# Regrouped filter rows, DMA transposes, normalization on ScalarE and smaller first blocks in a fused spectral and gated-FFN kernel

## The chip, the cores and the metric

The kernel runs on one core of one Trainium2 chip. The metric is the device time of one execution in microseconds (us). A time quoted for a kernel is the median of its runs. A profile is one execution with the hardware profiler on. Its span, from the first to the last instruction, is about 2 us shorter than the device time of the same execution.

The engines are PE (TensorE, matrix multiplications), DVE (VectorE), ACT (ScalarE), POOL (GpSimd) and SP (SyncE, which here only issues DMAs). PEld stands for PE's weight loads. In this program PE writes its results to a memory called PSUM, and the other engines fetch them from there. A transfer *lands* when its data have arrived.

## The reference, cut to what matters

```python
def reference(A_x, A_w_r, A_w_i, B_x, B_w_gate, B_w_up, B_w_down):   # A_x: 1 x 2048 x 512
    xn = _layernorm(A_x)                           # over the last axis
    X  = rfft2(xn);  X = X * (w_r + 1j * w_i)      # filter: 2048 x 257
    spectral = irfft2(X).astype(bf16)
    g  = xn @ w_gate;  u = xn @ w_up               # 512 x 1792 each
    ffn = (gelu(g) * u) @ w_down                   # 1792 x 512
    return A_x + spectral + ffn
```

All tensors are bf16. The kernel computes the Fourier transforms as matrix multiplications with constant tables.

## The kernel before

The 2048 rows are 16 chunks of 128 rows. One *unit* of the FFN (`glu`) makes 128 of the 1792 hidden columns for a block of chunks: 4 matmuls into `g_ps`, 4 into `u_ps`, the gelu on ACT, the product `hT` on DVE. For a block of 4 chunks one unit takes PE about 1.73 us. The other work is placed between the units by a hand-made list of tasks, each with the moment (in us of ideal PE time) at which it is put into the program. An engine runs its own instructions one after the other, near the program's order but not exactly in it: the traces show some places changed (in after, DVE takes the statistics of chunks 2 and 3 before chunk 0's reciprocal, which the program has the other way round). An engine's order below is the one that the trace shows. Cuts are marked with `# ...`.

```python
def layernorm(c0, n):                      # for the n chunks from c0
    for j in range(n):
        nc.vector.bn_stats(out=stats[:, j, :], in_=x_t[:, c0 + j, :])
        nc.vector.bn_aggr(out=mv[:, j, :], in_=stats[:, j, :])
    if c0 < 4:
        nc.scalar.activation(out=rstd[:], in_=mv[:, :, 1], func=AF.Sqrt, bias=eps_t[:], scale=1.0)
        nc.vector.reciprocal(out=rstd[:], in_=rstd[:])
    else:
        rsqrt(rstd, mv[:, :, 1], n)        # 12 small DVE instructions
    for j in range(n):
        nc.vector.tensor_scalar(out=xn[:, c0 + j, :], in0=x_t[:, c0 + j, :],
                                scalar1=mv[:, j, 0:1], scalar2=rstd[:, j:j + 1],
                                op0=ALU.subtract, op1=ALU.mult)

def transposes(c0):                        # two chunks, on PE, copied out of PSUM by DVE
    tp = ps.tile([P, NE, 2, P], BF16, name="tp", tag="S", bufs=4)
    for e in range(NE):
        for j in range(2):
            nc.tensor.transpose(tp[:, e, j, :], xn[:, c0 + j, e * P:(e + 1) * P], ident)
    nc.vector.tensor_copy(out=xnT[c0 // 4][:, :, c0 % 4:c0 % 4 + 2, :], in_=tp[:])
# ...
```

The spectral part folds `xn` by symmetry (`fold`, DVE), transforms along the rows (`pstep` into `bp`, `dstep` into `dp`, `cstep` into `ep`, each a group of matmuls and a cast on ACT), and then, for each of 8 groups g of frequencies, filters on DVE. The filtered tile `F` is shuffled across partitions by four DMAs before PE takes it up again:

```python
def filt(g):
    # ... X from E; two multiplications by the filter's rows, tr and ti
    V.tensor_tensor(out=m1[:]..., in0=Xv, in1=tr, op=ALU.mult)             # 128x1024, L340
    V.tensor_tensor(out=m2[:]..., in0=Xv[:, ::-1], in1=ti, op=ALU.mult)    # 128x1024, L341
    # ... Y and F from them, on DVE
    for h in range(2):
        for r in range(2):
            nc.sync.dma_start(out=F2[64 * r:64 * r + 64, h], in_=F[64 * h:64 * h + 64, r])   # L364
    f_tiles[g] = F2

def icstep(g):                             # back-transform: needs F2
    # ... per half: 4 matmuls into gp, then a cast on ACT to Gs
```

The filter rows are loaded as 28 plain loads and 18 gathers into `TW = [P, 2, NG, 2, 258]`. The program's order:

```python
layernorm(0, 2); transposes(0)
units = [(0, 2, fc) for fc in range(3)]          # the first 4 chunks in blocks of two
for fc in range(NFC):
    units.append((2, 2, fc))
    if fc + 3 < NFC: units.append((0, 2, fc + 3))
for sb in range(1, NSB):
    units += [(4 * sb, 4, fc) for fc in range(NFC)]
tasks = [(0, lambda: layernorm(2, 2)), (0, lambda: transposes(2))]
for cg in range(1, 4):
    t = 4 + 6 * (cg - 1)                         # layernorm at t, its transposes at t + 3
    # ...
for cg in range(4):
    t = 8 + 5 * cg                               # fold at t, the four psteps at t + 2 .. t + 5
    # ...
t0, dt = 32, 6.0
for g in range(NG):
    # dstep at t0 + dt*g and + 1, cstep and filt at + 4
    tasks.append((t0 + dt * g + 11, lambda g=g: icstep(g)))
# ... the units in order, each preceded by the tasks that are due;
# then idstep (into yp) and down (into y_ps), chunk by chunk
```

Of the kernel before, what the change touches and what calls it, by code (L numbers as in the profile page):

```python
# [10 lines left out]
P = 128  # L11
BF16 = mybir.dt.bfloat16
F32 = mybir.dt.float32
# [7 lines left out]
NG = 8  # L21
# [7 lines left out]
def _tables():  # L29
# [14 lines left out]
    p = np.arange(P)[:, None]  # L44
    ka = np.arange(64)[None, :]
    RF = np.zeros((P, NC, 2, 64))
# [49 lines left out]
    RI = np.zeros((2, 64, NC, P))  # L96
    kac = np.arange(64)[:, None]
    pr = np.arange(P)[None, :]
# [6 lines left out]
    def low(a):  # L105
        return a.reshape(P, -1).astype(np.float32).astype(ml_dtypes.bfloat16)


    h, kb, a = np.arange(P) // 64, np.arange(P) // 4 % 16, np.arange(P) % 4
    idx = np.zeros((P, NG, 2), dtype=np.int32)  # L110
    for g in range(NG):
        ks = 8 * g + 4 * h + a + 128 * kb
        if g == 0:
            ks = np.where((h == 0) & (a == 0) & (kb >= 8), 64 + 128 * (kb - 8), ks)
        idx[:, g, 0] = ks
        idx[:, g, 1] = (S - ks) % S
    idx[0, 0, 1] = S // 2
    return low(np.concatenate(parts, axis=1)), cols, low(RF), low(RI), idx.reshape(P, -1)


@with_exitstack
def kernel(
# [36 lines left out]
    late = {}  # L159
    TW = pc.tile([P, 2, NG, 2, 258], BF16, name="TW", tag="TW")  # L160
    TR, TI = TW[:, 0], TW[:, 1]
# [5 lines left out]
    def load_consts(first, last):  # L167
        a, b = ccols[first][0], sum(ccols[last])
        nc.sync.dma_start(out=CT[:, a:b], in_=cap[:, a:b])


    def load_x(c0, n, eng=nc.sync):
        eng.dma_start(out=x_t[:, c0:c0 + n, :], in_=x_v[:, c0:c0 + n, :])

    def load_w(a, b):
        nc.sync.dma_start(out=Wg_sb[:, :, a:b], in_=wg_v[:, :, a:b])
        nc.sync.dma_start(out=Wu_sb[:, :, a:b], in_=wu_v[:, :, a:b])

    load_x(0, 1)
    load_x(1, 1, nc.scalar)  # L180
    load_consts("ident", "ident")
    load_x(2, 2, nc.scalar)
    load_w(0, 256)
    load_w(256, 640)
    load_x(4, 4)
    load_w(640, 1216)
    load_x(8, 4)
    nc.sync.dma_start(out=RF_t[:], in_=rf_d.rearrange("p (c k) -> p c k", c=NC))
    load_w(1216, 1792)
    load_x(12, 4)  # L190
    load_consts("F0", "M0")




    W = 257
    idx_t = pc.tile([P, NG, 2], I32, name="idx_t")
    nc.gpsimd.dma_start(out=idx_t[:], in_=nc.inline_tensor(idx_np, name="spec_rows").ap()
                        .rearrange("p (g s) -> p g s", s=2))
    for T, w_in in ((TR, A_w_r), (TI, A_w_i)):  # L200
        rows = w_in.rearrange("(kb g h a) k -> h g kb a k", kb=NC, h=2, a=4)
        for g in range(NG):
            for s in range(2):
                if g > 0 and s == 0:
                    for h in range(2):
                        nc.sync.dma_start(out=T[64 * h:64 * h + 64, g, 0, 0:W], in_=rows[h, g])
                else:
                    nc.gpsimd.indirect_dma_start(
                        out=T[:, g, s, 0:W], out_offset=None, in_=w_in[:, :],
                        in_offset=bass.IndirectOffsetOnAxis(ap=idx_t[:, g, s:s + 1], axis=0))  # L210
    nc.sync.dma_start(out=Wd_sb[:], in_=wd_v)

# [24 lines left out]
    def layernorm(c0, n):  # L237
        stats = pw.tile([P, n, nc.vector.BN_STATS_DIM], F32, name="stats")
        mv = pw.tile([P, n, nc.vector.BN_AGGR_DIM], F32, name="mv")
        rstd = pw.tile([P, n], F32, name="rstd")  # L240
        for j in range(n):
            nc.vector.bn_stats(out=stats[:, j, :], in_=x_t[:, c0 + j, :])  # L242
            nc.vector.bn_aggr(out=mv[:, j, :], in_=stats[:, j, :])
        if c0 < 4:
            nc.scalar.activation(out=rstd[:], in_=mv[:, :, 1], func=AF.Sqrt, bias=eps_t[:], scale=1.0)
            nc.vector.reciprocal(out=rstd[:], in_=rstd[:])
        else:
            rsqrt(rstd, mv[:, :, 1], n)
        for j in range(n):
            nc.vector.tensor_scalar(out=xn[:, c0 + j, :], in0=x_t[:, c0 + j, :],  # L250
                                    scalar1=mv[:, j, 0:1], scalar2=rstd[:, j:j + 1],
                                    op0=ALU.subtract, op1=ALU.mult)

    def transposes(c0):
        tp = ps.tile([P, NE, 2, P], BF16, name="tp", tag="S", bufs=4)
        for e in range(NE):
            for j in range(2):
                nc.tensor.transpose(tp[:, e, j, :], xn[:, c0 + j, e * P:(e + 1) * P], ident)  # L258
        nc.vector.tensor_copy(out=xnT[c0 // 4][:, :, c0 % 4:c0 % 4 + 2, :], in_=tp[:])

# [26 lines left out]
    def evac(o, i):  # L287
        nc.scalar.copy(out=o, in_=i)  # L288
# [3 lines left out]
    def dstep(G):  # L292
        dp = ps.tile([P, 2, P, 2], F32, name="dp", tag="S", bufs=4)
        for q in range(4):
            nc.tensor.matmul(dp[:, q % 2, :, q // 2], lhsT=Bs[:, q, G].rearrange("p c r a -> p (c r a)"),  # L295
                             rhs=FQ[q], start=(q == 0), stop=(q == 3), skip_group_check=True)
        ds = pw.tile([P, D], BF16, name="ds", bufs=4)
        evac(ds[:], dp[:].rearrange("p s k t -> p (s k t)"))
        ds_tiles[G] = ds
# [14 lines left out]
    def tables_fix():  # L314
        V = nc.gpsimd
        t0 = pc.tile([1, 2, 2], BF16, name="t0")
        V.tensor_scalar(out=t0[0:1, 0, :], in0=TR[0:1, 0, :, 0], scalar1=0.5, scalar2=None, op0=ALU.mult)
        V.tensor_scalar(out=t0[0:1, 1, :], in0=TR[0:1, 0, :, 256], scalar1=0.5, scalar2=None, op0=ALU.mult)
        tt = pc.tile([P, 4, NG], F32, name="tt")
        V.tensor_tensor(out=tt[:, 0], in0=TR[:, :, 0, 0], in1=TR[:, :, 1, 0], op=ALU.add)  # L320
        V.tensor_tensor(out=tt[:, 1], in0=TR[:, :, 0, 256], in1=TR[:, :, 1, 256], op=ALU.add)
        V.tensor_tensor(out=tt[:, 2], in0=TI[:, :, 0, 0], in1=TI[:, :, 1, 0], op=ALU.subtract)
        V.tensor_tensor(out=tt[:, 3], in0=TI[:, :, 0, 256], in1=TI[:, :, 1, 256], op=ALU.subtract)
        for k, (T, s) in enumerate(((TR, 0), (TR, 1), (TI, 0), (TI, 1))):
            V.tensor_scalar(out=T[:, :, s, 0], in0=tt[:, k], scalar1=0.5, scalar2=None, op0=ALU.mult)
        f_tiles["t0"] = t0

    def filt(g):
# [5 lines left out]
        V.tensor_copy(out=X[:, :, 0].rearrange("p (r s) -> p r s", r=2), in_=E[:, :, :, 0])  # L334
        tr = TR[:, g, :, 0:256].unsqueeze(1).to_broadcast([P, 2, 2, 256])
        ti = TI[:, g, :, 0:256].unsqueeze(1).to_broadcast([P, 2, 2, 256])
        m1 = pw.tile([P, 4, 256], BF16, name="m1", bufs=1)
# [12 lines left out]
        if g == 0:  # L350

            u = pw.tile([1, 2, 2, 256], BF16, name="u", tag="A", bufs=1)
            E0, F0 = E[0:1], F[0:1]
            TR0, TI0 = TR[0:1, 0, :, 0:256], TI[0:1, 0, :, 0:256]
            for s, op in ((0, ALU.add), (1, ALU.subtract)):
# [13 lines left out]
    def icstep(g):  # L369
        F = f_tiles[g]  # L370
        if g == 0:
            late["G"] = pc.tile([P, 4, NC, 2, 64], BF16, name="Gs", tag="x_t")
# [73 lines left out]

    layernorm(0, 2)
    transposes(0)
    units = [(0, 2, fc) for fc in range(3)]
    for fc in range(NFC):  # L450
        units.append((2, 2, fc))
        if fc + 3 < NFC:
            units.append((0, 2, fc + 3))
    for sb in range(1, NSB):
        units += [(4 * sb, 4, fc) for fc in range(NFC)]

    tasks = [(0, lambda: layernorm(2, 2)), (0, lambda: transposes(2))]

    for cg in range(1, 4):
        t = 4 + 6 * (cg - 1)  # L460
        tasks.append((t, lambda cg=cg: layernorm(4 * cg, 4)))
        tasks.append((t + 3, lambda cg=cg: transposes(4 * cg)))
        tasks.append((t + 3, lambda cg=cg: transposes(4 * cg + 2)))
    for cg in range(4):
        t = 8 + 5 * cg
        tasks.append((t, lambda cg=cg: fold(cg)))
        for q in range(4):
            tasks.append((t + 2 + q, lambda cg=cg, q=q: pstep(cg, q)))
    tasks.append((20, tables_fix))
    t0, dt = 32, 6.0  # L470
    for g in range(NG):
        tasks.append((t0 + dt * g, lambda g=g: dstep(2 * g)))
        tasks.append((t0 + dt * g + 1, lambda g=g: dstep(2 * g + 1)))
        tasks.append((t0 + dt * g + 4, lambda g=g: cstep(g)))
        tasks.append((t0 + dt * g + 4, lambda g=g: filt(g)))
        tasks.append((t0 + dt * g + 11, lambda g=g: icstep(g)))
    tasks.sort(key=lambda x: x[0])
# [45 lines left out]
```

## Time and profile before

| | before |
|---|---|
| device time, median of 3 runs | 198.14 us (198.07 to 198.33) |
| device time of the profiled run | 217.64 us |
| first `g_ps` matmul in that profile | 9.85 us |
| PE, busy share of the profiled span | 85% |

These are lines of the profile's page for the kernel before. A row has 40 digits, one for each fortieth of the span. A digit is the busy share in tenths. PEclk is the granted TensorE clock in tenths of full speed.

```profile
span 215.6 us, 3193 instructions
...
PE   0581009999889999999999899999999999999993
...
PEclk9998555999999999999999999999999999999999
```

PE is nearly full after a poor start. There is a hole in slices 4 to 6, with the clock at half in slices 5 to 7. This profiled run was 19.5 us longer than the timed ones, so it isn't the timed program.

The chain of waits of the kernel before, near its start (start in us, duration in us, what):

```profile
3.73 1.29 DVE stats L242 x2
...
9.85 1.01 PE g_ps L425 x4
...
16.21 15.92 another core or an unknown queue x2
```

The data of the first chunks land at 3.7 us, and the first FFN matmul starts 6.1 us later. The last line is the hole: 15.9 us that no recorded instruction explains.

The same profile in stretches: the window, its length, then busy us and (instructions) of PE, PEld, DVE, ACT and POOL, the clock, the busy share of the DMA engines, GB/s.

```profile
40.00:50.00 10.00, 9.52 (x97) 7.98 (x96) 9.64 (x33) 4.81 (x12) 0.82 (x4) 1.00 0.66 219
50.00:63.00 13.00, 11.05 (x109) 8.85 (x108) 12.79 (x46) 5.67 (x14) 0.00 (x0) 1.00 0.01 2
```

From 40 to 63 us DVE is busy for 22.4 of 23 us, while PE has gaps. This is the stage with layernorm, fold and the copies of the transposes.

One line from the list of PE's waits (what waited, on what: us in total, times, longest), and one multiplication by the filter's rows of each kind (line, engine, operation, tiles, shapes, count; then busy us, mean ns, and idle us before it):

```profile
PE gp L378 <- DMA F_1361<-F: 0.6, 2, 0.4
```

```profile
L340 DVE TENSOR_TENSOR m_950<-X,TW 128x1024 bf16<-128x1024 bf16 x1 | 0.7, 694 | 0.0
...
L341 DVE TENSOR_TENSOR m_1054<-X,TW 128x1024 bf16<-128x1024 bf16 x1 | 0.7, 686 | 0.0
```

PE waits for the shuffle of F.

### The profile page before, as it was taken

How to read it: one execution, taken by the hardware profiler on the slowest of the kernel's cores; microseconds unless marked ns; L12 is line 12 of the kernel's file. 1: busy time of each engine (PE TensorE's matmuls, PEld its weight loads, DVE VectorE, ACT ScalarE, POOL GpSimd, SP SyncE). 2: the span in 40 equal slices, each digit the busy share in tenths (PEclk: the TensorE clock that was granted, in tenths of full speed). 3: DMA queues.
4: the chain of work that ended last, by engine and by line, in shares of the span. 5: the costliest groups of instructions: out<-in, count | busy, mean ns of one | idle time of the engine just before them, and what ended most of it. 6: DMA issues, size and time to landing. Idle time of an engine off the chain costs nothing.

```text
span 215.6 us, 3193 instructions
## 1 busy us (share of the span) xinstructions
PE 184.0 (85%) x1136; PEld 102.2 (47%) x1136; DVE 126.2 (59%) x316; ACT 90.3 (42%) x170; POOL 20.3 (9%) x33
## 2 busy tenths in 40 slices
PE   0581009999889999999999899999999999999993
PEld 0451006787665545455445445444454444545441
DVE  3970006999998339978578487493353544255421
ACT  2310002353618566787778768754341212121100
POOL 1777740100000000000000000000000000000000
PEclk9998555999999999999999999999999999999999
DMA  5999732760000200101202202202002222222211
GB/s 166 362 382 380 205 76 49 223 213 3 0 2 3 97 0 2 41 19 40 49 0 52 50 0 55 49 0 49 0 3 73 73 73 85 70 91 72 77 49 49
DMA packets 17503, 17.69 MB, mean 82 GB/s; under 512 B 2208, under 2 KB 16304, under 8 KB 17488
## 3 DMA queue, kind: packets, MB, share of 16 engines
q1 hardware_dynamic: 16592, 15.90, 24.1%
q0 software_dynamic: 608, 1.19, 1.9%
q10 hardware_dynamic: 288, 0.39, 0.6%
q8 instruction: 9, 0.15, 0.3%
q14 instruction: 6, 0.05, 0.1%
HBM read 13.29 MB, written 2.10 MB: 71 GB/s over the span
## 4 chain that ended last, share of the span: by engine, by line
PE 57%; DVE 17%; another core or an unknown queue 7%; issue 6%; DMA 5%; ACT 5%; SPq 2%; DVEq 0%
PE y_ps L438 22%; PE u_ps L428 12%; PE g_ps L425 12%; ACT E L310 3%; DVE stats L242 2%; SPq L364 2%; PE tp L258 2%; DVE hT_187 L432 2%; PE dp L295 2%; PE yp L393 2%; PE y_ps L440 2%; DMA x_t<-in_A_x_dram 1%; PE bp L282 1%; DVE hT_1164 L432 1%
## 5 line engine op out<-in xcount | busy, mean ns | idle before, releaser
L431 ACT ACTIVATE ge<-g_ps 128x512 bf16<-128x512 f32 (+1 forms) x70 | 35.4, 517 | 52.2 <-PE g_ps L425 26.3
L428 PEld LDWEIGHTS <-Wu_sb 128*128 128x128 bf16 x280 | 28.3, 101 | 35.2 <-issue 14.9
L425 PEld LDWEIGHTS <-Wg_sb 128*128 128x128 bf16 x280 | 28.6, 104 | 23.2 <-issue 5.2
L443 DVE TENSOR_TENSOR y_sb<-y_ps,y_sb 128x512 bf16<-128x512 f32 x16 | 11.1, 692 | 30.2 <-PE y_ps L440 30.2
L425 PE MATMUL g_ps<-xnT_70,Wg_sb 128*128 128x256 bf16 x112 | 19.4, 300 | 10.5 <-issue 10.5
L428 PE MATMUL u_ps<-xnT_70,Wu_sb 128*128 128x256 bf16 x112 | 18.5, 297 | 7.8 <-DVE hT_187 L432 7.0
L399 ACT CAST yf<-yp 128x512 bf16<-128x512 f32 x16 | 9.2, 587 | 37.3 <-PE yp L393 37.3
L432 DVE TENSOR_TENSOR hT_187<-u_ps,ge 128x256 bf16<-128x256 f32 x28 | 11.6, 419 | 19.6 <-remote 16.0
L310 ACT CAST E<-ep 64x512 bf16<-64x512 f32 x32 | 18.5, 579 | 4.0 <-PE ep L307 3.7
L425 PE MATMUL g_ps<-xnT_72,Wg_sb 128*128 128x512 bf16 x56 | 15.4, 384 | 0.0
L425 PE MATMUL g_ps<-xnT_71,Wg_sb 128*128 128x512 bf16 x56 | 15.0, 381 | 0.0
L425 PE MATMUL g_ps<-xnT_73,Wg_sb 128*128 128x512 bf16 x56 | 14.9, 380 | 0.0
L428 PE MATMUL u_ps<-xnT_72,Wu_sb 128*128 128x512 bf16 x56 | 14.9, 379 | 0.0
L428 PE MATMUL u_ps<-xnT_73,Wu_sb 128*128 128x512 bf16 x56 | 14.9, 379 | 0.0
L428 PE MATMUL u_ps<-xnT_71,Wu_sb 128*128 128x512 bf16 x56 | 14.4, 380 | 0.0
L432 DVE TENSOR_TENSOR hT_807<-u_ps,ge 128x512 bf16<-128x512 f32 x14 | 9.6, 687 | 7.0 <-PE u_ps L428 6.7
L258 PE MATMUL tp<-CT,xn 128*128 128x128 bf16 x64 | 6.5, 243 | 7.7 <-DVE xn L250 7.6
L438 PE MATMUL y_ps<-Wd_sb,hT_187 128*128 128x512 bf16 x56 | 12.7, 379 | 0.0
L438 PE MATMUL y_ps<-Wd_sb,hT_807 128*128 128x512 bf16 x56 | 12.7, 379 | 0.0
L438 PE MATMUL y_ps<-Wd_sb,hT_1164 128*128 128x512 bf16 x56 | 12.7, 379 | 0.0
L242 DVE BATCH_NORM_STATS2 stats<-x_t 128x6 f32<-128x512 bf16 x16 | 10.6, 678 | 3.4 <-DMA x_t<-in_A_x_dram 3.4
L288 ACT CAST Bs<-bp 128x512 bf16<-128x512 f32 x16 | 8.5, 598 | 6.3 <-PE bp L282 6.3
(126 smaller groups left out, 242.0 us busy)
## 6 DMA issues: line engine op xcount, KB each, us to landing
y_sb<-in_A_x_dram SPq DMA_DIRECT2D x16, 128.0 KB
out_dram<-y_sb SPq DMA_DIRECT2D x16, 128.0 KB
Wd_sb<-in_B_w_down_dram SPq DMA_DIRECT2D x1, 1792.0 KB
x_t<-in_A_x_dram SPq DMA_DIRECT2D x3, 512.0 KB
Wg_sb<-in_B_w_gate_dram SPq DMA_DIRECT2D x2, 576.0 KB
Wu_sb<-in_B_w_up_dram SPq DMA_DIRECT2D x2, 576.0 KB
RF_t<-spec_rf SPq DMA_DIRECT2D x1, 512.0 KB
RI_t<-spec_ri SPq DMA_DIRECT2D x1, 512.0 KB
```

The source lines that it names most:

```text
L242: nc.vector.bn_stats(out=stats[:, j, :], in_=x_t[:, c0 + j, :])
L258: nc.tensor.transpose(tp[:, e, j, :], xn[:, c0 + j, e * P:(e + 1) * P], ident)
L288: nc.scalar.copy(out=o, in_=i)
L295: nc.tensor.matmul(dp[:, q % 2, :, q // 2], lhsT=Bs[:, q, G].rearrange("p c r a -> p (c r a)"), rhs=FQ[q], start=(q == 0), stop=(q == 3), ...
L310: nc.scalar.copy(out=E[64 * h:64 * h + 64, r], in_=ep[64 * r:64 * r + 64])
L399: nc.scalar.copy(out=yf[:, c % 2], in_=yp[:])
L425: nc.tensor.matmul(gp[:], lhsT=Wg_sb[:, e, fc * P:(fc + 1) * P], rhs=rhs[:, e, :], start=(e == 0), stop=(e == NE - 1))
L428: nc.tensor.matmul(up[:], lhsT=Wu_sb[:, e, fc * P:(fc + 1) * P], rhs=rhs[:, e, :], start=(e == 0), stop=(e == NE - 1))
L431: nc.scalar.activation(out=ge[:], in_=gp[:], func=AF.Gelu_apprx_tanh)
L432: nc.vector.tensor_tensor(out=hT[sb, fc][:, o:o + w], in0=up[:], in1=ge[:], op=ALU.mult)
L438: nc.tensor.matmul(y_ps[:], lhsT=hT[sb, f][:, cl * P:(cl + 1) * P], rhs=Wd_sb[:, f, :], start=(f == 0), stop=False)
L443: nc.vector.tensor_tensor(out=y_sb[:], in0=y_ps[:], in1=y_sb[:], op=ALU.add)
```

## The change

Its intent is to take work from PE (48 of 64 transposes) and from DVE (the normalization of 12 chunks and the copies of their transposes), to start PE earlier with one-chunk blocks, and to replace 46 small table loads by 10 larger ones. The schedule is rewritten too. The core of the diff, cut:

```diff
-    TW = pc.tile([P, 2, NG, 2, 258], BF16, name="TW", tag="TW")
+    TW = pc.tile([P, 2, 17, W], BF16, name="TW", tag="TW")          # W = 257
@@ tables: 28 loads and 18 gathers become
+        for T, w_in in ((TR, A_w_r), (TI, A_w_i)):
+            Tf = T.rearrange("p j k -> p (j k)")
+            rows = w_in.rearrange("(kb a h g) k -> h kb a (g k)", kb=NC, h=2, a=8)
+            for h in range(2):
+                nc.sync.dma_start(out=Tf[64 * h:64 * h + 64, W:8 * W], in_=rows[h, :, 0:4, W:8 * W])
+            gather(Tf[:, 8 * W:16 * W], w_in.rearrange("(n r) k -> n (r k)", r=8), 2)
+        # ... and two gathers of one row per partition for each table
@@ first loads: the first weights now stand before x of chunks 2 and 3
     load_x(1, 1, nc.scalar)
+    load_w(0, 256, nc.scalar)
     load_consts("ident", "ident")
     load_x(2, 2, nc.scalar)
-    load_w(0, 256)
@@ layernorm
-        if c0 < 4:                                 # sqrt on ACT
+        if c0 < 2:
@@
+        if c0 >= 4:
+            nb = ...                               # -mean * rstd, one small DVE instruction
+            # and per chunk, in place of DVE's tensor_scalar:
+            nc.scalar.activation(out=xn[:, c0 + j, :], in_=x_t[:, c0 + j, :], func=AF.Identity,
+                                 bias=nb[:, j:j + 1], scale=rstd[:, j:j + 1])
@@ transposes, for chunks 4 to 15
+            for j in range(c0, c0 + n):
+                nc.sync.dma_start_transpose(out=xnT[j // 4][:, :, j % 4, :], in_=xn[:, j, :])
@@ the layout of dp in PSUM
-        dp = ps.tile([P, 2, P, 2], F32, name="dp", tag="S", bufs=4)
+        dp = ps.tile([P, 2, 2, P], F32, name="dp", tag="S", bufs=4)
-            nc.tensor.matmul(dp[:, q % 2, :, q // 2], lhsT=Bs[:, q, G]..., rhs=FQ[q], ...)
+            nc.tensor.matmul(dp[:, q // 2, q % 2, :], lhsT=Bs[:, q, G]..., rhs=FQ[q], ...)
@@ order of the program
+    units = [(c, n, fc) for c, n in ((0, 1), (1, 1), (2, 2)) for fc in range(4)]
+    units += [(0, 4, fc) for fc in range(4, NFC)]
-        t = 4 + 6 * (cg - 1)                       # layernorm
+        t = 8 + 8 * (cg - 1)
-        t = 8 + 5 * cg                             # fold
+        t = 8 + 8 * cg
-    t0, dt = 32, 6.0
-    for g in range(NG):                            # ... cstep, filt at + 4
-        tasks.append((t0 + dt * g + 11, lambda g=g: icstep(g)))
+    t0, dt = 42, 5.5
+    for i, g in enumerate((1, 2, 3, 4, 5, 6, 7, 0)):   # ... cstep, filt at + 3
+        tasks.append((t0 + dt * i + 12, lambda g=g: icstep(g)))
```

Not shown: the permutation of the Fourier tables that goes with the new grouping, the new slices in `filt` and `tables_fix`, how the weights are cut into loads, and the later moments of the table loads and of the load of `w_down`.

## The prediction

> **What bounds the kernel now.** The profile of before is not the timed program: the profiled execution took 217.64 us, the timed ones 198.14. The excess, 19.5 us, has one visible home: in the chain of waits, 16.2 to 32.1 us is 15.9 us on "another core or an unknown queue", while engines idle, matmul and DMA records are missing, and the clock drops to 0.5. I read the stall as made by profiling under the early flood of DMA packets (250 to 390 GB/s until 23 us, in the table of stretches), and don't count it as time to win.
>
> What remains, a span of about 196 us:
> - PE: by the columns of all matmuls, 167 us at full clock (FFN 143, spectral 20.5, 64 transposes 3.4). From 156 us to the end it is gapless (y_ps).
> - Start: first g_ps matmul at 9.85 us, behind x landing at 3.7 and layernorm and transposes of two chunks.
> - 40 to 63 us: DVE is busy 22.4 of 23 us; PE did columns for 17.5. DVE bounds this stage (layernorm, fold, PSUM copies, hT); about 5 us lost.
> - 63 to 156 us: PE loses 7 to 8 us in small waits (ACT E and Gs casts, hT).
>
> **What the change does.**
> 1. One-chunk first blocks: g_ps needs one chunk's layernorm, 4 transposes and a 512-column copy. Wg, Wu and the identity land near 6.3 us as before. First g_ps at about 7.6: -2.2 us. Eight one-chunk units are bound by weight loads: +0.6.
> 2. 48 of 64 PE transposes go (0.053 us each at full clock): -2.6 us of PE.
> 3. DVE loses 12 xn (0.41 us each) and 6 to 7 copies of 0.69, and gains nb and one more rsqrt chain: about -7 us of some 44 us through the last fold. The DVE-bound stage becomes nearly PE-bound: -3 us. ACT gains 12 Identity ops of about 0.55 us, so it is 80 to 90% busy there; some of it returns as late gelu.
> 4. Twelve DMA transposes of 128 KB. The Trainium skill, "DMA: Bandwidth & Descriptors", "Latency and other measured facts", gives 261 GB/s in one kernel; no trace here has one. Estimate 1 to 3 us each with landing, issued several us before first use: off the path, the main risk.
> 5. Tables: 28 loads (about 0.6 us of SP issue each) and 18 gathers (0.95 us of POOL each) become 4 and 6. They were off the critical path: nothing in the timed run.
> 6. The rows' pitch goes from 258 to 257 elements, so odd rows are not 4-byte aligned. "VectorE: DVE Perf Modes", "Mode 2×_1P", asks for 4-byte alignment. The filter multiplications (0.69 us for 128x1024) should rise to about 1.15 for odd g: 8 x 0.46 = 3.7 us of DVE, where it is 70% busy: +0.5 us.
> 7. The denser spectral schedule (5.5 for 6) and g=0 last: the last filter, its DMA and icstep arrive just before idstep: 0 to +2 us.
>
> Sum: -2.2 +0.6 -2.6 -3 +0.5 +0.5 and some ACT pressure: about -7.
>
> **Prediction: 191.0 us, range 185.5 to 197.0.** Faster by over 2%: 0.77; within: 0.17; slower: 0.06.
>
> **Right or wrong, in the profile.** First g_ps near 7.6; DVE under 90% in the stage before the last fold; no g_ps waiting for a DMA transpose; filter multiplications in two durations by parity of g; gapless y_ps. The early stall should shrink, so that the profiled time falls by more than the timed one.
>
> **What would make it wrong.** DMA transposes of 5 us or more, or holding SP's queue; ACT late with gelu behind Identity ops; weights landing late without the profiler too; a bubble before idstep.

## The result, and the profile after

| | before | after |
|---|---|---|
| median of 4 runs of the same rounds | 198.24 us (198.07 to 198.45) | 193.36 us (192.99 to 193.78) |
| ratio, 95% interval | | 0.9754 (0.9726 to 0.9782) |
| profiled run | 217.64 us | 192.99 us |
| first `g_ps` in the profile | 9.85 us | 10.28 us |

A ratio is the mean time of one kernel's runs over that of the other's runs of the same rounds, so it is not quite the ratio of the medians. Executions over 1.5% slower than the fastest of the same kernel are left out of the means. The change is faster by 4.9 us. Seven were predicted, and 193.36 lies inside the predicted range.

PE's row of the page, for the kernel after:

```profile
PE   0098998999999998989989979997999999999992
```

The hole is gone. What is left are small losses, most of them in slices 17 to 28, between about 76 and 134 us.

The same profile in stretches, columns as above:

```profile
10.00:20.00 10.00, 9.19 (x104) 8.07 (x103) 9.89 (x40) 3.37 (x11) 0.00 (x0) 1.00 1.06 383
20.00:30.00 10.00, 9.90 (x59) 5.13 (x60) 10.00 (x40) 6.45 (x11) 5.12 (x6) 1.00 0.95 254
30.00:40.00 10.00, 9.28 (x54) 4.66 (x54) 9.14 (x32) 8.17 (x16) 3.32 (x11) 1.00 1.21 267
40.00:50.00 10.00, 9.95 (x59) 5.04 (x59) 7.00 (x12) 8.48 (x16) 0.00 (x0) 1.00 0.75 120
```

DVE is still full from 10 to 30 us and has room only after that. ACT is now over 80% busy between 30 and 50 us.

PE's waits in the kernel after, the longest ones (what waited, on what: us in total, times, longest):

```profile
PE tp L272 <- DVE xn L260: 9.1, 1, 9.1
PE gp L396 <- DMA F_901<-F: 1.1, 2, 0.7
PE gp L396 <- DMA F_1376<-F: 1.0, 2, 0.7
PE yp L411 <- ACT Gs L305: 0.9, 1, 0.9
PE g_ps L443 <- ACT ge L449: 0.7, 1, 0.7
```

The first is the start. With the five shorter waits on F that are left out, `gp` waits 4.1 us in all for shuffles of F. No `g_ps` waits for a DMA transpose. After the start, the wait for F is the largest.

The start, from the order of DVE's instructions (start, duration, engine, line, operation, tiles and shapes, count; in brackets the idle time before, and what ended it):

```profile
4.01 1.29 DVE L247 BATCH_NORM_STATS2 stats<-x_t 128x6 f32<-128x512 bf16 x2 [3.15 <-DMA x_t<-in_A_x_dram]
...
7.25 1.29 DVE L247 BATCH_NORM_STATS2 stats<-x_t 128x6 f32<-128x512 bf16 x2 [1.73 <-DMA x_t<-in_A_x_dram]
8.45 0.15 DVE L251 RECIPROCAL rstd<-rstd 128x1 f32<-128x1 f32 x1
8.63 0.41 DVE L260 TENSOR_SCALAR xn<-x_t,mv,rstd 128x512 bf16<-128x512 bf16 x1
```

ACT has the square root of chunk 0 ready by 5.9 us. But the statistics of chunks 2 and 3 stand in front of chunk 0's reciprocal in DVE's order (the program's text has them behind it), and their x lands only at 7.25 us, because the weights are now loaded first. So DVE idles for 1.73 us with work for chunk 0 behind it. The Trainium skill, "PSUM — Partial Sum Buffer", section "Engine vs sequencer instructions", says that "ScalarE/VectorE/GpSimdE queues are strict FIFO" (first in, first out). This trace agrees: the reciprocal's input was ready by 5.9 us, and it ran at 8.45 us, behind those statistics.

The path of one group g through the shuffle, in the chain of waits of the kernel after:

```profile
72.39 0.42 DVE F L366
...
73.53 0.53 SPq L382
...
74.75 0.59 SPq L382
...
75.38 2.03 DMA F_901<-F
...
77.54 0.40 PE gp L396 x4
```

SP issues the shuffle's DMAs one after the other at about 0.6 us each, and the last one, 64 KB within the core's memory SBUF, then takes 2.03 us to land. The chain has this sequence once for each of several groups g. The skill's "DMA: Bandwidth & Descriptors", section "Latency and other measured facts", speaks of a DMA fixed cost of about 2 us and puts it down mostly to HBM, the chip's main memory. The 2.03 us here come close to that figure, though this transfer doesn't touch HBM.

The end of that stage, in the same chain:

```profile
128.33 2.03 DMA F_1573<-F
...
130.50 0.40 PE gp L396 x4
...
130.92 1.08 ACT Gs L305 x2
...
132.05 0.84 PE yp L411 x12
```

The last `gp` now stands directly before `yp`, so PE waits through its casts. That is the predicted bubble. From `y_ps` on both kernels take the same: 54.87 us after (132.73 to 187.60), and 54.87 us in before_again, an undisturbed profile of before (see the experiments).

One more difference stands in the traces, and neither the prediction nor an experiment looks at it: the matmuls into `dp`. The chain of waits in before_again, and then in after:

```profile
63.67 0.87 PE dp L295 x8
```

```profile
84.71 0.22 PE dp L312 x4
```

In before such a matmul writes every second element of `dp`, in after adjacent ones. One of them (128 columns) takes 0.109 us in before and 0.055 us in after, so all 64 take 7.0 and 3.5 us of PE. The regrouped tables are not the reason: b_tables has them with the old layout, and its pace is 0.109 us too. What these 3.4 us of PE's time are worth in the time of the kernel no run shows, since none changes the layout alone.

The multiplications by rows at an odd pitch, the longest and the shortest of all 16:

```profile
L358 DVE TENSOR_TENSOR m_1257<-X,TW 128x1024 bf16<-128x1024 bf16 x1 | 0.7, 697 | 0.0
...
L359 DVE TENSOR_TENSOR m_891<-X,TW 128x1024 bf16<-128x1024 bf16 x1 | 0.7, 681 | 0.0
```

The longest eight (691 to 697 ns) are one line of the program and the other eight (681 to 690 ns) another, as in before. Within a line the parity of g makes no second duration.

The normalization on ACT, in the groups (columns as for the multiplications), and the DMA transposes (the durations of their issue in ns, min/median/max; at the end the time to landing in us, for the four of xnT_71):

```profile
L264 ACT ACTIVATE xn<-x_t,nb,rstd 128x512 bf16<-128x512 bf16 x12 | 8.8, 813 | 1.0 <-DVE nb L256 1.0
```

```profile
L276 SPq DMA_TRANSPOSE xnT_71<-xn x4: 1200/1254/2782, 27.1 to 31.8; - x4
...
DMA to landing us min/median/max: 4.2/5.0/7.9
```

### The profile page after: what moved, and what is told of

The parts are those of the page before. It is cut to its first block, busy times and chain, and to the rows that moved or that the text cites. A ratio compares the mean times of both kernels' runs of the same rounds, so it can differ in the third digit from the quotient of the medians.

```text
span 191.2 us, 2960 instructions
## 1 busy us (share of the span) xinstructions
PE 171.0 (89%) x1022; PEld 88.5 (46%) x1040; DVE 119.2 (62%) x308; ACT 97.2 (51%) x176; POOL 8.6 (5%) x20
## 4 chain that ended last, share of the span: by engine, by line
PE 40%; DMA 6%; DVE 6%; SPq 4%; issue 3%; ACT 2%; DVEq 0%
PE y_ps L456 25%; PE g_ps L443 4%; SPq L382 4%; PE u_ps L446 4%; PE y_ps L458 2%; PE yp L411 2%; PE gp L396 1%; DVE hT_1591 L450 1%; DMA F_1376<-F 1%; DMA F_984<-F 1%; DMA F_1573<-F 1%; DMA F_1079<-F 1%; DMA F_901<-F 1%; DMA F_1174<-F 1%; DVE hT_926 L450 1%
## 5 line engine op out<-in xcount | busy, mean ns | idle before, releaser
L449 ACT ACTIVATE ge<-g_ps 128x512 bf16<-128x512 f32 (+2 forms) x64 | 34.7, 550 | 25.5 <-PE g_ps L443 23.2
L446 PEld LDWEIGHTS <-Wu_sb 128*128 128x128 bf16 x256 | 24.6, 99 | 25.2 <-issue 0.6
L443 PEld LDWEIGHTS <-Wg_sb 128*128 128x128 bf16 x256 | 23.5, 100 | 19.3 <-issue 1.1
L443 PE MATMUL g_ps<-xnT_70,Wg_sb 128*128 128x512 bf16 (+2 forms) x85 | 16.1, 311 | 1.3 <-ACT ge L449 0.7
L446 PE MATMUL u_ps<-xnT_70,Wu_sb 128*128 128x512 bf16 (+2 forms) x88 | 16.1, 310 | 0.3 <-DVE hT_157 L450 0.2
L450 DVE TENSOR_TENSOR hT_623<-u_ps,ge 128x512 bf16<-128x512 f32 x14 | 9.6, 689 | 10.9 <-PE u_ps L446 10.9
L443 PE MATMUL g_ps<-xnT_72,Wg_sb 128*128 128x512 bf16 x54 | 14.6, 379 | 0.1
L443 PE MATMUL g_ps<-xnT_73,Wg_sb 128*128 128x512 bf16 x53 | 14.4, 379 | 0.1
L446 PE MATMUL u_ps<-xnT_71,Wu_sb 128*128 128x512 bf16 x56 | 14.4, 379 | 0.1
L446 PE MATMUL u_ps<-xnT_73,Wu_sb 128*128 128x512 bf16 x56 | 14.4, 379 | 0.0
L446 PE MATMUL u_ps<-xnT_72,Wu_sb 128*128 128x512 bf16 x55 | 14.3, 379 | 0.1
L443 PE MATMUL g_ps<-xnT_71,Wg_sb 128*128 128x512 bf16 x53 | 14.1, 379 | 0.1
L305 ACT CAST Gs<-gp 128x512 bf16<-128x512 f32 x16 | 9.2, 587 | 6.4 <-PE gp L396 6.4
L450 DVE TENSOR_TENSOR hT_157<-u_ps,ge 128x512 bf16<-128x512 f32 (+2 forms) x22 | 10.6, 489 | 0.0
L305 ACT CAST ds<-dp 128x512 bf16<-128x512 f32 x16 | 9.3, 588 | 1.5 <-PE dp L312 1.5
```

The source lines that it names most:

```text
L305: nc.scalar.copy(out=o, in_=i)
L443: nc.tensor.matmul(gp[:], lhsT=Wg_sb[:, e, fc * P:(fc + 1) * P], rhs=rhs[:, e, :], start=(e == 0), stop=(e == NE - 1))
L446: nc.tensor.matmul(up[:], lhsT=Wu_sb[:, e, fc * P:(fc + 1) * P], rhs=rhs[:, e, :], start=(e == 0), stop=(e == NE - 1))
L449: nc.scalar.activation(out=ge[:], in_=gp[:], func=AF.Gelu_apprx_tanh)
L450: nc.vector.tensor_tensor(out=hT[sb, fc][:, o:o + w], in0=up[:], in1=ge[:], op=ALU.mult)
```

## The experiments

All outputs are right. Each table row gives the median, the range, and the ratio to before of the same rounds. The kernel after was not run again in these rounds. So a difference to after is taken from ratios: (ratio minus 0.9754) times 198.3 us. The intervals of the ratios are about 0.001 to 0.003 to either side. Since the interval of after itself comes on top, a difference to after of less than about 0.9 us is not clear of noise.

| kernel | median us (range) | ratio (95% interval) | against after, us |
|---|---|---|---|
| tables alone, on before (b_tables) | 197.67 (197.51 to 197.75) | 0.9978 (0.9965 to 0.9992) | |
| x of chunks 2, 3 first (a_x23_early) | 194.04 (192.85 to 194.93) | 0.9784 (0.9752 to 0.9817) | +0.6 |
| all transposes on PE (a_pe_transpose) | 195.36 (195.19 to 195.68) | 0.9865 (0.9849 to 0.9881) | +2.2 |
| normalization on DVE (a_dve_norm) | 192.11 (191.86 to 192.34) | 0.9701 (0.9686 to 0.9716) | -1.1 |
| later icstep, on after (a_ic_late) | 188.78 (188.09 to 189.04) | 0.9510 (0.9488 to 0.9532) | -4.8 |
| two-chunk first blocks (a_old_blocks) | 192.60 (192.02 to 195.01) | 0.9716 (0.9684 to 0.9748) | -0.8 |
| schedule of before (a_old_sched) | 195.89 (194.75 to 196.66) | 0.9867 (0.9837 to 0.9897) | +2.2 |
| combination (best1) | 185.33 (185.05 to 185.46) | 0.9339 (0.9321 to 0.9358) | -8.2 |
| before, profiled again (before_again) | 198.25, one run | | |
| later icstep, on before (b_ic_late) | 195.13 (194.87 to 195.56) | 0.9842 (0.9824 to 0.9860) | |
| combination with the start mended (best2) | 184.50 (183.54 to 185.14) | 0.9294 (0.9268 to 0.9320) | -9.1 |
| combination, transposes on PE (best1_pe_tr) | 189.58 (189.44 to 189.72) | 0.9557 (0.9541 to 0.9573) | +4.3 against best1 |

A second table says where PE's time went before the last stage. The columns are the first `g_ps`, the first `yp` (where the back-transform of the last stage starts), and what PE lost between the two. For the loss I priced the columns of all matmuls in between, as the program has them, at the steady rate of the traces (0.216 us for 512 columns), and took that from the time between the two moments. It is an accounting with an uncertainty of some tenths of a us. The slow matmuls into `dp` are priced at the full rate too, so in the rows of before_again and b_ic_late 3.4 us of "lost" are theirs.

| profile of | first g_ps | first yp | columns priced | lost |
|---|---|---|---|---|
| before_again | 9.7 | 137.3 | 113.2 | 14.3 |
| b_ic_late | 9.8 | 133.9 | 113.2 | 10.9 |
| after | 10.3 | 132.1 | 111.0 | 10.8 |
| a_dve_norm | 10.0 | 130.9 | 111.0 | 9.9 |
| a_x23_early | 8.9 | 133.3 | 111.0 | 13.4 |
| a_ic_late | 10.1 | 127.9 | 111.0 | 6.8 |
| best1_pe_tr | 10.1 | 128.8 | 113.6 | 5.0 |
| best1 | 10.0 | 124.5 | 111.0 | 3.5 |

From before to after: 0.6 us later at the start, 2.2 us fewer columns, 3.5 us less lost. That gives the 5.2 us by which the first `yp` comes earlier, against 4.9 us in the times. The pace of `dp` alone is 3.4 of the 3.5 us: what else PE lost less in one place, it lost more in another (see the end).

### b_tables: the regrouped tables alone, on the kernel before

```diff
 # before, with the table hunks of the change (index, TW, loads, slices) and nothing else
-    for T, w_in in ((TR, A_w_r), (TI, A_w_i)):      # 28 loads, 18 gathers
-        # ...
+    load_tables()                                   # 4 loads, 6 gathers, at the same place
     nc.sync.dma_start(out=Wd_sb[:], in_=wd_v)
```

> Before, with the regrouped tables alone (4 loads and 6 gathers, issued where before issues its 28 and 18). Theory 1 (the tables were off the path, and the 16 us stall in the profile of before is made by profiling): timed within 0.7 us of before, about 198.2, yet the profiled execution drops from 217.6 to within 3 us of the timed one. Rival (the small table DMAs also slow the timed start): 194 or less, that is, this part is most of the gain.

It measured 0.2% less than before, about 0.4 us. The tables were off the path, as predicted. Its profile has no stall, which looked like a point for the theory that the many small table DMAs make the stall under the profiler. The next experiment takes that point back.

### before_again: the kernel before, unchanged, profiled a second time

```diff
 (no edit)
```

> Before, unchanged, profiled once more. Theory (its 16 us stall is made by profiling, where many small table DMAs run under the early flood): the profiled execution is again 8 us or more over the timed ones, with engines idle together between 15 and 33 us. Rival (the stall was one chance event): a profiled execution near 198 us with no such stall.

The profiled run took 198.25 us, with a span of 196.2 us and a clock of 1.00, and the hole is not there. It lies within the range of the 11 runs of before on the same chip, 198.0 to 198.84. PE's waits in this profile:

```profile
PE tp L258 <- DVE xn L250: 7.7, 2, 7.2
PE u_ps L428 <- DVE hT L432: 2.0, 4, 0.8
PE gp L378 <- DMA F<-F: 1.8, 6, 0.4
```

Its stretches from 30 to 50 us (columns as above), for comparison with those of after:

```profile
30.00:40.00 10.00, 8.70 (x90) 6.93 (x89) 10.00 (x34) 5.03 (x12) 0.84 (x4) 1.00 0.24 49
40.00:50.00 10.00, 9.18 (x85) 6.24 (x85) 9.52 (x28) 4.81 (x11) 0.81 (x4) 1.00 0.72 229
```

So the stall of the first profile is not a property of this program under the profiler. It happened in one of two profiled executions. My reason for it, the flood of small DMAs, fell. What made it stays open. Not counting it as time to win was right. All comparisons of traces below use this second profile.

### a_x23_early: x of chunks 2 and 3 before the first weights, on after

```diff
     load_x(1, 1, nc.scalar)
+    load_x(2, 2, nc.scalar)
     load_w(0, 256, nc.scalar)
     load_consts("ident", "ident")
-    load_x(2, 2, nc.scalar)
```

> After, with chunks 2 and 3 of x loaded before the first weights on the ACT queue. Theory (the first g_ps is at 10.28 us instead of 7.6 because the statistics of chunks 2 and 3 stand in DVE's order before the reciprocal of chunk 0, and wait for their x until 7.2 us): reciprocal near 6.7, first g_ps at 8.4 to 9.1, and the timed run 1 to 2 us under after, about 192. Rival (weights or the identity set the start): the first g_ps stays at 10 or goes later, and the time does not fall.

The first `g_ps` came at 8.87 us, 1.41 us earlier, but the time did not fall (194.04 us; the 0.6 us above after are not clear of noise). PE at that place, instructions in order:

```profile
10.52 0.79 PE L443 MATMUL g_ps<-xnT,Wg_sb 128*128 128x128 bf16 x8
12.81 0.38 PE L446 MATMUL u_ps<-xnT,Wu_sb 128*128 128x128 bf16 x4 [1.49 <-DVE hT L450]
```

PE then stands for 1.5 us, until 12.81 us: it needs the first `hT`, and in DVE's order the statistics of chunks 4 to 7 stand in front of it, waiting for their x until 10.08 us. The first `hT` starts at 12.47 us, against 12.65 us in after. So the earlier start is lost again while the second wait in DVE's queue is there. This profile also has a wait of 1.1 us for a gelu at 41.5 us that after lacks, so its later end doesn't price the start alone.

### a_old_blocks: the first four chunks as two blocks of two, on after

```diff
-        if c0 < 2:
+        if c0 < 4:
@@
-    for c in range(2):
-        layernorm(c, 1)
-        transposes(c, 1)
+    layernorm(0, 2)
+    transposes(0, 2)
     layernorm(2, 2)
     transposes(2, 2)
-    units = [(c, n, fc) for c, n in ((0, 1), (1, 1), (2, 2)) for fc in range(4)]
+    units = [(c, n, fc) for c, n in ((0, 2), (2, 2)) for fc in range(4)]
```

> After, with first blocks of two chunks (layernorm and transposes of 2 and 2, units of two chunks) as before. Theory (the start is bound by DVE's order, not by the size of the first block): within 0.8 us of after, 192.6 to 194.2. Rival (smaller first blocks gain the 1.6 us that were predicted, and something else lost it): 194.7 to 195.5.

The time was 192.6 us, 0.8 us less than after by the ratios, whose intervals overlap slightly. Undoing the one-chunk blocks cost nothing, so no gain from them shows. Its profiled run counts as slow (195.01 us), so I read only its first 21 us, where the clock is 1.00: the first `g_ps` comes 1.1 us later than in after (11.39 us), and PE still reaches its first four-chunk unit at 20.25 us, against 20.37 us.

### a_dve_norm: the normalization of all chunks on DVE, on after

```diff
-        if c0 >= 4:
+        if False:                       # no nb
@@
-            if c0 < 4:
+            if True:                    # DVE tensor_scalar for all chunks
```

> After, with the normalization of chunks 4 to 15 on DVE as before. Theory (DVE is full from 10 to 40 us, so 12 times 0.41 us come back there and part of it is exposed): 1 to 3 us over after, 194.5 to 196.5. Rival (ACT, 84% busy from 30 to 50 us, lost as much as DVE won): within 0.7 us of after or under it.

It was faster than after by 1.1 us: moving the normalization to ACT was a loss. The stretches of this kernel, to be compared with the last two of after:

```profile
30.00:40.00 10.00, 10.00 (x60) 5.02 (x59) 10.00 (x35) 5.23 (x9) 4.86 (x11) 1.00 1.04 248
40.00:50.00 10.00, 10.00 (x60) 5.05 (x59) 9.25 (x22) 5.42 (x10) 0.79 (x2) 1.00 1.12 186
```

DVE is full, and PE has no gap at all. A full DVE did no harm, because the work that filled it was not needed soon. On ACT the four normalizations of a group stand together in front of the next gelu (2.93 us in a row at 26.3 us in after), and PE stops for that gelu. An operation cost 0.41 us on DVE (median 406 ns in this run) and 0.81 us on ACT.

That duration could have been known. The skill's "ScalarE: Activation LUTs", section "What ACT_TABLE_LOAD costs", gives 186 ns + 0.833 ns per element, about 93 ns more for each pointer operand, and an overlap of about 93 ns when they follow one another. For two pointers and 512 elements this gives an estimate of 799 ns. The trace of after has 797 to 844 ns, and (2.93 - 0.81)/3 = 0.71 us from one to the next. The prediction had put it at 0.55 us.

### a_pe_transpose: all transposes on PE, on after

```diff
-        if c0 < 4:
-            # ... PE transposes
-        else:
-            for j in range(c0, c0 + n):
-                nc.sync.dma_start_transpose(out=xnT[j // 4][:, :, j % 4, :], in_=xn[:, j, :])
+        for k in range(c0, c0 + n, min(n, 2)):
+            # ... PE transposes in pairs of chunks, and a DVE copy out of PSUM for each pair
```

> After, with PE transposes and copies out of PSUM for all chunks instead of DMA transposes. Theory (DMA transposes are off the path and save PE 2.6 us and DVE 6 copies of 0.69 us where DVE is full): 2.6 to 5 us over after, 196 to 198. Rival (their latency of 2.4 to 7.9 us and the SP time of 1.2 us each cost as much as they save): within 1 us of after.

It was 2.2 us slower by the ratios (2.0 by the medians), just under the range expected. The 48 transposes are 2.6 us of PE's columns. So in after their removal gives about what PE saves and no more: the DVE copies that went with them were not what PE waited for there.

### best1_pe_tr: the same edit on best1 (below)

The diff is the one just shown, on best1.

> best1, with PE transposes for all chunks. In best1 PE has no gaps, so the transposes' own PE time must show: 48 times 0.053 is 2.6 us, so 187.6 to 188.6, and up to 2 us more if the six copies on DVE, full until 50 us, are exposed. Rival (DMA transposes cost SP and DMA time that is exposed): under 2 us.

It was 4.3 us slower than best1: above the range of 187.6 to 188.6 us, within the further 2 us that the expectation allows. Of this, 2.6 us are columns. The rest is lost time (5.0 against 3.5 us in the table), in which PE waits for `xn` in front of transposes (1.4 us by my count of gaps). Where DVE normalizes and copies, and nothing else holds PE, the DMA transposes are worth more than in after.

### a_ic_late and b_ic_late: one number, the moment of icstep

```diff
 # a_ic_late, on after
-        tasks.append((t0 + dt * i + 12, lambda g=g: icstep(g)))
+        tasks.append((t0 + dt * i + 15, lambda g=g: icstep(g)))
```

> After, with each icstep (gp) queued 15 instead of 12 units of schedule time behind its dstep, so that 7 instead of 5 FFN units stand between ep and gp in PE's order. Theory (in the spectral stage PE, in order, stops at gp for the four shuffle DMAs of F: ten gaps of 0.5 to 1.1 us in the trace of after, 5.8 us beyond a usual step): the gaps go and the time falls by 3.5 to 5.5 us, to 188 to 190. Rival (the stage is bound by ACT and DVE, and gp is only where PE happens to wait): under 1 us, the gaps turn up at g_ps or u_ps.

```diff
 # b_ic_late, on before
-        tasks.append((t0 + dt * g + 11, lambda g=g: icstep(g)))
+        tasks.append((t0 + dt * g + 15, lambda g=g: icstep(g)))
```

> Before, with icstep 15 instead of 11 behind its dstep and nothing else. Theory (the waits at gp for the shuffle DMAs were in before already, eleven gaps of 0.4 to 0.7 us in the twin with regrouped tables, and the change left them in): 2 to 4 us under before, 194.2 to 196.2, so one number gives about half of what the whole change gave. Rival (before is bound there by DVE and ACT): within 1 us of before.

On after the number is worth 4.8 us (188.78 us), on before 3.1 us by the ratio (195.13 us). The whole change is worth 4.9 us. PE's waits in a_ic_late, all that are left after the start:

```profile
PE g_ps L443 <- ACT xn L264: 1.2, 1, 1.2
PE yp L411 <- ACT Gs L305: 0.9, 1, 0.9
PE g_ps L443 <- ACT ge L449: 0.7, 1, 0.7
PE g_ps L443 <- DVE xnT L273: 0.6, 1, 0.6
```

No `gp` waits for F. The list counts only time in which no record of a matmul is open, and a record (379 ns for 512 columns) outlasts the 216 ns to the next start, so it hides part of each gap. By the starts of the matmuls, PE lost 5.8 us in front of `gp` in after and nothing in a_ic_late, where the new wait of 1.2 us takes some of it back; on before, 3.9 us (before_again) and 0.9 us (b_ic_late). These differences match the gains of 4.8 and 3.1 us.

In after, five units stand between a `cstep` and its `icstep`, about 8.6 us of PE's time; the way through the casts, DVE's filter, the issue of the DMAs and their landing takes longer than that. With seven units it fits. The skill's DMA page, "Rules for kernel authors", row "Overlap DMA with compute", says the same in general: issue early, wait late. The runs put a price on it.

### a_old_sched: before's schedule, on after

```diff
-    tasks = [(20, load_tables)]
+    tasks = [(8, load_tables)]
-        t = 8 + 8 * (cg - 1)
+        t = 4 + 6 * (cg - 1)
-        t = 8 + 8 * cg
+        t = 8 + 5 * cg
-    tasks.append((36, tables_fix))
-    t0, dt = 42, 5.5
-    for i, g in enumerate((1, 2, 3, 4, 5, 6, 7, 0)):
+    tasks.append((20, tables_fix))
+    t0, dt = 32, 6.0
+    for g in range(NG):                 # cstep, filt at + 4; icstep at + 11
```

> After, with the schedule of before (layernorms every 6 and folds every 5, dsteps from 32 at a pitch of 6, icstep 11 behind, g in order 0 to 7; tables loaded at 8). Theory A (spreading layernorm and fold over a longer stretch took the DVE-bound loss away): 1.5 to 3.5 us over after. Theory B (the new schedule has longer waits at gp and a bubble of 1.2 us before idstep, so the old one is as good): within 1 us of after or under it.

It was 2.2 us slower by the ratios. So the new schedule is a gain, not a cost. Part of the 2.2 us goes with the clock: three of the six runs have a mean clock of 0.988 to 0.991 and took 196.25 to 196.66 us, the other three (0.996 to 1.0) took 194.75 to 195.54 us, which is 1.7 us above after. The profile is one of the first three; its clock is 0.50 from 40 to 42 us, just after PE's idle time before `bp`. The waits of `gp` for F are the same with either (4.0 us here, 4.1 us in after), so they are not its doing. The chain of waits of this kernel shows where the old one loses:

```profile
28.31 6.30 DMA xnT<-xn
34.60 2.20 ACT xn L264 x3
...
36.83 0.69 DVE A L286
...
39.51 0.71 PE bp L299 x8
```

The fold (`A`, `xf`) comes due while ACT is still normalizing its chunks, and PE stands at `bp` for 2.2 us (its list of waits puts it down to ACT's `xn`). The chain also puts a DMA transpose, 6.30 us to landing, in front of that normalization. ACT has no idle time there, and whether it needed that landing I did not test. The new schedule spreads layernorm and fold 8 us apart instead of 6 and 5. The gain holds for a kernel that normalizes on ACT; on before the schedule alone was not tried.

### best1: what the experiments point to

```diff
 # after, with the edit of a_dve_norm, and
-    tasks.append((36, tables_fix))
-    t0, dt = 42, 5.5
+    tasks.append((34, tables_fix))
+    t0, dt = 38, 5.5
-        tasks.append((t0 + dt * i + 12, lambda g=g: icstep(g)))
+        tasks.append((t0 + dt * i + 16, lambda g=g: icstep(g)))
```

> After, with normalization back on DVE, dsteps from 38 instead of 42 and icstep 16 behind instead of 12. If the effects add: -1.25 (measured for the normalization alone) and -4.5 (gaps at gp) and -1 (bubble before idstep): 186.5 to 188. If they overlap: 189 to 191.

It ran in 185.33 us, better than either theory had it. PE's waits in its profile, all of them:

```profile
PE tp L272 <- DVE xn L260: 8.8, 1, 8.8
PE g_ps L443 <- DVE xnT L273: 0.6, 1, 0.6
```

After the start one wait of 0.6 us is left. The bubble before `yp` is gone because the last `gp` now stands two units earlier. The parts add up to 5.9 us (1.1 for the normalization, 4.8 for icstep), and it gained 8.2 us; the rest goes with the earlier `t0` and with the parts' interplay, which I did not take apart further.

### best2: best1 with both waits of the start removed

```diff
     load_x(1, 1, nc.scalar)
+    load_x(2, 2, nc.scalar)
     load_w(0, 256, nc.scalar)
-    load_x(2, 2, nc.scalar)
@@
-        if c0 < 2:
+        if c0 < 4:                      # sqrt on ACT for chunks 2 and 3 too
@@ each hT instruction is kept in the list hts (not shown); the order of DVE's queue
+    def behind(n, work):                # work is put behind the n-th hT in the order of issue
+        with tc.issue_after(hts[n].ins):
+            work()
-        tasks.append((t, lambda cg=cg: layernorm(4 * cg, 4)))
+        tasks.append((t, lambda cg=cg: behind(3 if cg == 1 else len(hts) - 3, lambda: layernorm(4 * cg, 4))))
-        tasks.append((t, lambda cg=cg: fold(cg)))
+        tasks.append((t, lambda cg=cg: behind(5 if cg == 0 else len(hts) - 3, lambda: fold(cg))))
```

> best1, with chunks 2 and 3 of x loaded before the weights, the ACT square root for them too, and chunk 4's layernorm and the first fold queued in DVE's order behind the fourth and sixth hT. Theory (an early first g_ps gains only if DVE's order lets the first hT through as well): first g_ps at 8.5 to 9.1 us, no gap over 0.5 us in the first 20 us, and 0.8 to 1.8 us under best1, 183.5 to 184.5. Rival (the work on DVE, not its order, sets the start): within 0.4 us of best1.

It ran in 184.50 us, 0.9 us less than best1 by the ratios. The first `g_ps` came at 8.74 us, and this time no gap of more than 0.5 us follows in the first 20 us. Of the 1.3 us won at the start, part is given back: PE waits three times in front of `bp`, since the fold now stands later in DVE's order (0.7 us in the list of waits). This is the fastest of all kernels, 7.1% under before.

## Why the prediction was right or wrong

The total was about right, 193.36 us against 191.0 us, but partly through terms that were wrong in opposite directions, which is luck. (The terms as listed add up to -6.2 us, not to "about -7"; -4.9 was measured.) The start was not won (-1.6 us predicted in all), and the waits for the shuffle grew by 1.9 us; against these stand 3.4 us of PE's time from the layout of `dp`, which the prediction doesn't mention. That the profiled time fell by more than the timed one, as predicted, was chance too: the stall did not come back in before_again.

1. **"One-chunk first blocks: ... First g_ps at about 7.6: -2.2 us" was wrong, and it is the step that failed most plainly.** The first `g_ps` came at 10.28 us, 0.4 us later than in before's first profile. The estimate followed chunk 0's own dependencies and left out what stands before them in DVE's queue: the statistics of chunks 2 and 3, whose x the same change loads later. (Before was misread as well: its first `g_ps` stands behind the transposes of four chunks, 16 from 7.15 us on in before_again, not of two.) The runs showed that removing this wait alone brings the first `g_ps` to 8.87 us and no time (a_x23_early); there the first `hT` stands behind other statistics. Only when both are removed is there a gain, 0.9 us (best2). Undoing the blocks costs nothing (a_old_blocks). "Bound by weight loads: +0.6" did not show either: from 13 us on, 128-column matmuls of one-chunk units start every 0.056 us in after, in step with their columns.
2. **"48 of 64 PE transposes go: -2.6 us of PE" was right.** It measured 2.2 us in after, and 4.3 us in best1.
3. **"The DVE-bound stage becomes nearly PE-bound: -3 us" held in its size more than in its reason.** By the starts of matmuls, PE stood in front of `u_ps`, `tp`, `bp` and `g_ps` for about 4.1 us between 20 and 63 us in before_again, and for 0.8 us in after. DVE's busy time fell by 6.9 us over the run (126.1 us in before_again, 119.2 us in after), as predicted. But it did not fall under 90% before the last fold: it is 9.9 and 10.0 of 10 us from 10 to 30 us. And the part of it that was moved to ACT cost 1.1 us. What the runs show to help, in a kernel that normalizes on ACT, is the wider spacing of layernorm and fold: going back to the old schedule costs 2.2 us, of which part is a lower clock. How much of the 3 us each part brought is open. The ACT operation was mis-sized, 0.55 us for a measured 0.81. The warning that "some of it returns as late gelu" was right.
4. **The DMA transposes stayed off the path, as predicted.** They took 2.4 to 7.9 us to land (median 4.5), not 1 to 3, but they were issued early enough. No `g_ps` waits for one.
5. **The tables were worth nothing, nearly as predicted:** 0.4 us.
6. **The alignment term (+0.5 us) was wrong.** The multiplications take 681 to 697 ns for every g, as before. The page that the prediction relied on has a counterpart in the same skill that says the opposite (see the last section), and it was not looked up.
7. **"The denser spectral schedule ...: 0 to +2 us" was right about the bubble**: 0.9 us before `yp`, which a_old_sched doesn't have. The schedule as a whole is a gain of 2.2 us, but a_old_sched also undoes the spacing of layernorm and fold, and its trace shows the loss there. The spectral part alone was not tried.
8. **What the prediction did not see** are the two largest things in the traces. Its reading "63 to 156 us: PE loses 7 to 8 us in small waits (ACT E and Gs casts, hT)" has other parts: in before, 3.9 us stand in front of `gp`, for the shuffle of F, which the list of waits names, and 3.4 us are the slow pace of `dp`. The change removes the second and lets the first grow to 5.8 us. One number in the schedule, which takes the wait for F away, is worth 3.1 us in before and 4.8 us in after.

Adding up the single parts by the ratios (transposes -2.2, normalization +1.1, first blocks +0.8, schedule -2.2, tables -0.4) gives -2.9 us, against 4.9 us measured. The parts depend on each other, and the order of the loads, the layout of `dp` and the later load of `w_down` were not tried alone. So 2 us are not assigned. The layout of `dp` is the likely place, with 3.4 us of PE's time in the traces, but a run of before with this edit alone would have to show it.

Also open: what stalled the first profile of before, and whether the shuffle itself could be made shorter (fewer DMAs, or issued from two engines) instead of being given more time.

## What to carry to other kernels

Before you give an engine less work, ask what PE waits for: a full DVE cost nothing here when its work was not due, and a transfer awaited two units too soon cost as much as the whole change gained. Follow a start through each engine's queue, in the order that a trace shows, not through the dependencies of the first tile alone. Compare the pace of every group of matmuls before and after, not only the waits. A move from one engine to another is priced on the new engine and at its place in that engine's order.

## What the Trainium skill lacked or had wrong

- "VectorE: DVE Perf Modes", section "Mode 2×_1P", requires 4-byte alignment. In after half of the 16 multiplications of 128x1024 bf16 have rows that start 2 bytes off a 4-byte boundary; all 16 took 681 to 697 ns, the aligned ones of before 684 to 694 ns. "Vector Engine (DVE) Microarchitecture Reference", section 5.1, has it right ("4-byte alignment makes no difference"); the two pages contradict each other.
- "DMA: Bandwidth & Descriptors", section "Latency and other measured facts", gives a bandwidth for the DMA transpose (261 GB/s) but no time from issue to landing for a single one. For 128 KB within SBUF it was a median of about 1.2 us of SP's issue and 2.4 to 7.9 us to landing.
- The same page, section "Issuing engines are not separate DMA queues", calls the time to initiate a DMA "usually small relative to the DMA itself". In the shuffle of F it was not: four DMAs at 0.46 to 0.60 us each, some 2.3 us in a row, against 2.03 us for the last one to land.
- No page that I read shows what a strict order costs at a kernel's start. Here it was 1.73 us of an idle DVE, with ready work for chunk 0 behind statistics whose data had not landed.
- No page that I found gives the pace of a matmul that writes every second element of PSUM. For 128 columns it was 0.109 us, against 0.055 us for adjacent elements.
